# Gated linear attention and a soft mixture of experts on one core: first block by halves, a new schedule table

## The chip, the cores and the metric

The kernel runs on one core of a Trainium2 chip. A core has five engines that work beside each other, each through its own list of instructions in order: TensorE (PE, with its weight loads as PEld), VectorE (DVE), ScalarE (ACT), GpSimd (POOL) and SyncE (SP), which here issues all DMA transfers. The metric is device time in microseconds of one execution; the time before is 164.95 us, the median of 3 runs (164.65 to 165.14).

## What is computed

```python
# _attn_ref: B, H, S, D = 4, 8, 768, 48
f = 1.0 / (1.0 + np.exp(-f_logit))
for t in range(S):
    state = f[:, :, t, :, None] * state + k[:, :, t] outer v[:, :, t]
    y[:, :, t] = q[:, :, t] times state
# y is reordered to x: 3072 x 384
# _moe_ref: 8 experts of 4 slots, F = 1024
logits = x @ phi                       # 3072 x 32
d = softmax of logits over the tokens
slot_input = d.T @ x                   # 32 x 384
slot_out[e] = np.maximum(slot_input[e] @ w1[e], 0.0) @ w2[e]
c = softmax of logits over the slots
return c @ slot_out                    # 3072 x 384
```

(The two lines of the loop and the two softmax lines are shortened.) Everything is 32-bit floating point.

## The kernel before

**Blocks.** The attention is cut into 24 blocks (`NN`): 6 stretches of 128 time steps for each of 4 batches, all 8 heads of a batch in one block. The decay inside a block is turned into running sums of logarithms, so that a block is a few matrix products and a state handed on to the block four later.

**Gates** (`gates`, lines 478 to 506). ACT takes exp (L495, with a sum of its outputs kept for a flag, which costs an ACTIVATION_READ_ACCUMULATOR) and ln (L498) of the gate inputs; DVE scans each block in two runs of 256 columns (L487, L488); ACT takes exp of the sums (`g`, L501) and of their negatives (`p`, L502). Blocks 0 and 1 have gates of 512 columns each, later ones 1024 for a pair of blocks.

**Block** (`block`, L508 on). Two multiplies of 512 columns, `mk` (keys by `g`, L524) and `mq` (queries by `p`, L527), on POOL or DVE; `tk` turns the keys (L532, four transposes), `pk` evicts them (L535), `kv` (L553) builds the block's share of the state, `sa` and `sm` (L557, L562) add and scale it; `ie` (L572) applies the old state to the queries, `sc` (L541) makes the scores, `mask` (L544, DVE) masks them, `ia` (L581) applies them to the values, `py` (L584) evicts. `turn_y` turns the result (`tx` L612, `px` L615). Every fourth block `unit` adds logits, the token softmax in running form, and the slots' inputs (L630 to L665).

**Tail.** From the last unit the slots' inputs are summed (`psi` L752, evicted by DVE as `si` L757); then come `up` (L788), relu, turning, `dn` (L822), a sum over experts (`so` L834) and the combination with the other softmax (`cb` L845), in three parts of the columns; `pf` (L854 to L859) copies the result for the stores. `slots` makes the softmax over the slots (L699 to L714).

**A flag.** The fast way is right only where the gates stay in bounds. `flag1` (five DVE operations, L898 to L902), `flag2` (a transpose, L905) and `flag3` (three small DVE operations, L908 to L910) reduce that to one number; at the end every engine reads it and branches over a slow general version.

**Start.** While the first loads land, eight steps called `warm` (L426) keep TensorE busy, each of two products of 128 x 128 ones (two records a product in the trace).

**The order.** The program has no order written by hand. Each step is given to a planner (`Plan`) with its possible engines and their planned durations, the tiles that it reads and writes, and a due time (`prio`). `schedule` simulates the engines: again and again it takes the step that can begin first; among steps that could begin within `WINDOW` of each other the lower `prio` wins. The list that comes out is the program's order on all engines, the loads on SP's queue included. The table `LATER` shifts due times by kind of step and by an index; `ENGINE` fixes the engine of some kinds (A ACT, D DVE, P POOL, - or an engine that the step can't use: free choice). The index is the first number in the step's name, below 4 as it stands, above that 4 + x % 4:

```python
            x = x if x < 4 else 4 + x % 4
            op["prio"] += LATER[kind][x] if kind in LATER else 0.0
            e = ENGINES[ENGINE[kind][x]] if kind in ENGINE else None
```

The planner's model also has a price for a change of the kind of product on TensorE (`SWITCH`), for every 256 instructions that TensorE fetches (`FETCH`), and a rate for DMA. None of these prices is a wait on the chip: only the order and the choice of engines go into the program.

## Time and profile before

| | us |
|---|---|
| median of 3 runs | 164.95 |
| the profiled execution, its own time | 164.98 |
| its span, first to last instruction | 163.2 |
| TensorE busy (x2461) | 147.3 |
| DVE busy (x234) | 120.3 |
| ACT busy (x186) | 99.0 |
| POOL busy (x43) | 26.2 |

The mean granted clock of TensorE is 0.987. Times of the profile are counted from the start of the span. Its rows give the start, the duration, the engine, the line of the kernel, the operation, output and inputs with their shapes, and a count; in brackets the time that the engine stood idle before it and what ended that. "PE" and "PEld" are products and weight loads of TensorE; a product of 32-bit numbers appears as two records. DMA moved 54.01 MB at a mean of 331 GB/s.

### The profile page before, as it was taken

What the parts mean: (1) busy time and instruction counts of PE and PEld (TensorE: products, weight loads), DVE (VectorE), ACT (ScalarE), POOL (GpSimd) and SP (SyncE); (2) the same over time, 40 slices, a digit from 0 to 9 for tenths busy, and PEclk for the clock granted to TensorE, in tenths of its full rate; (3) what the DMA queues carried; (4) which work ended last, traced back from release to release, by engine and by line L of the source; (5) the groups of instructions that cost most, each with busy time, mean ns of one, the idle gap of its engine ahead of it and who ended that gap; (6) DMA issues with size and microseconds to landing.
All of it is one profiled execution on the core that took longest, in us unless ns stands there. A gap on an engine that the chain in (4) does not pass through costs nothing.

```text
span 163.2 us, 5865 instructions
## 1 busy us (share of the span) xinstructions
PE 147.3 (90%) x2461; PEld 112.6 (69%) x2461; DVE 120.3 (74%) x234; ACT 99.0 (61%) x186; POOL 26.2 (16%) x43
## 2 busy tenths in 40 slices
PE   2998999999999999999999999999999999999600
PEld 2987777688877797878877887778753248777300
DVE  6789998899999999989999999999371113250410
ACT  4998977796959888783886967743440130033520
POOL 4001111050305020060306322160011000000000
PEclk9999999999999999999999999999999999999995
DMA  4999999999999799999999988618999998046891
GB/s 149 346 404 386 407 419 398 383 374 413 390 377 381 267 381 368 382 329 350 387 407 375 319 315 253 241 24 353 428 426 420 420 418 345 16 180 231 332 375 66
DMA packets 17571, 54.01 MB, mean 331 GB/s; under 512 B 1920, under 2 KB 5120, under 8 KB 14464
## 3 DMA queue, kind: packets, MB, share of 16 engines
q1 hardware_dynamic: 17536, 53.55, 87.0%
q8 instruction: 21, 0.34, 0.8%
q14 instruction: 14, 0.11, 0.2%
HBM read 48.82 MB, written 4.72 MB: 328 GB/s over the span
## 4 chain that ended last, share of the span: by engine, by line
PE 61%; DVE 14%; ACT 8%; DMA 7%; issue 3%; SPq 2%; POOL 1%; ACTq 0%; DVEq 0%; POOLq 0%
PE pr L541 12%; PE pr L581 6%; PE sg L612 6%; PE pr L572 5%; PE pr L788 5%; PE sg L822 5%; DVE as L544 4%; DMA ag<-in_f_dram 4%; PE sg L630 3%; PE sg L532 3%; PE pr L845 3%; DMA aq<-in_q_dram 3%; PE sg L659 2%; PE sg L553 2%; PE pr L822 2%
## 5 line engine op out<-in xcount | busy, mean ns | idle before, releaser
L544 DVE TENSOR_TENSOR as<-pr,tri 128x1024 f32<-128x1024 f32 x24 | 29.1, 1214 | 2.2 <-PE pr L541 1.5
L541 PE MATMUL pr<-aq,ak 48*128 48x128 f32 x384 | 27.9, 285 | 0.4 <-DVE as L544 0.2
L541 PEld LDWEIGHTS pr<-aq,ak 48*128 48x128 f32 x384 | 23.3, 187 | 5.0 <-issue 2.5
L581 PE MATMUL pr<-as,av 128*48 128x128 f32 x384 | 24.1, 274 | 1.2 <-DVE as L544 1.0
L581 PEld LDWEIGHTS pr<-as,av 128*48 128x48 f32 x384 | 20.2, 123 | 2.9 <-DVE as L544 2.1
L612 PE MATMUL sg<-ident,xT 128*128 128x128 f32 x96 | 15.2, 282 | 0.4 <-ACT ag L535 0.2
L527 POOL TENSOR_TENSOR aq<-aq,ac 128x512 f32<-128x512 f32 x9 | 11.4, 1281 | 25.0 <-ACT ac L502 8.7
L584 ACT COPY xT<-pr 128x512 f32<-128x512 f32 x20 | 11.5, 582 | 5.5 <-PE pr L581 5.4
L524 POOL TENSOR_TENSOR ak<-ak,af 128x512 f32<-128x512 f32 x6 | 7.7, 1279 | 35.3 <-ACT af L501 23.4
L572 PE MATMUL pr<-aq,st 48*48 48x128 f32 x320 | 13.1, 278 | 0.2 <-DVE aq L527 0.2
L502 ACT ACTIVATE ac<-ac 128x1024 f32<-128x1024 f32 (+1 forms) x13 | 12.9, 993 | 0.5
L612 PEld LDWEIGHTS sg<-ident,xT 128*128 128x128 f32 x96 | 10.4, 141 | 3.6 <-issue 1.5
L854 ACT COPY hm<-pr 128x768 f32<-128x768 f32 x7 | 5.5, 802 | 10.9 <-PE pr L845 10.9
L532 PE MATMUL sg<-ident,ak 128*128 128x128 f32 x80 | 11.9, 282 | 0.0
L487 DVE TENSOR_TENSOR_SCAN ac<-chain,af 128x256 f32<-128x256 f32 x16 | 10.9, 681 | 1.1 <-issue 1.1
L535 ACT COPY ag<-sg 128x512 f32<-128x512 f32 x17 | 9.4, 586 | 3.7 <-PE sg L532 3.7
L615 ACT COPY xr<-sg 128x384 f32<-128x384 f32 x17 | 8.1, 479 | 4.9 <-PE sg L612 4.8
L488 DVE TENSOR_TENSOR_SCAN ac<-chain,af 128x256 f32<-128x256 f32 x16 | 10.6, 665 | 0.0
L553 PEld LDWEIGHTS sg<-av,ag 128*48 128x48 f32 x320 | 8.6, 124 | 2.7 <-issue 1.2
L527 DVE TENSOR_TENSOR aq<-aq,ac 128x512 f32<-128x512 f32 x15 | 10.2, 685 | 0.3 <-POOL ak L524 0.2
L572 PEld LDWEIGHTS pr<-aq,st 48*48 48x48 f32 x320 | 8.0, 119 | 3.4 <-issue 2.0
L532 PEld LDWEIGHTS sg<-ident,ak 128*128 128x128 f32 x80 | 8.6, 141 | 2.2 <-issue 0.9
(142 smaller groups left out, 243.0 us busy)
## 6 DMA issues: line engine op xcount, KB each, us to landing
hm<-in_w_dram SPq DMA_DIRECT2D x17, 1024.0 KB, 8.0
ak<-in_k_dram SPq DMA_DIRECT2D x24, 256.0 KB, 5.9
aq<-in_q_dram SPq DMA_DIRECT2D x24, 256.0 KB, 5.8
av<-in_v_dram SPq DMA_DIRECT2D x24, 192.0 KB, 5.4
af<-in_f_dram SPq DMA_DIRECT2D x7, 512.0 KB, 5.6
out_dram<-hm SPq DMA_DIRECT2D x8, 384.0 KB, 3.8
ag<-in_f_dram SPq DMA_DIRECT2D x4, 512.0 KB, 5.9
out_dram<-hm SPq DMA_DIRECT2D x2, 768.0 KB, 4.3
```

The source lines that it names most:

```text
L487: nc.vector.tensor_tensor_scan(cx[:, : 2 * BT], chain, lx[:, : 2 * BT], 0.0, op0=ALU.mult, op1=ALU.add)
L502: add(f"p{n}", {"ACT": t_act(w)}, lambda e: nc.scalar.activation(flat(c_), flat(c_), AF.Exp, scale=-1.0), w=cs, prio=T(n, 1.2))
L527: tt(e)(flat(q_), flat(q_), flat(c_), op=ALU.mult)
L532: nc.tensor.transpose(pk[:, a], k_[:, a], ident)
L541: nc.tensor.matmul(ps[:, r, a], k_[rows[r], col(a)], queries(r, a), start=True, stop=True)
L544: tt(e)(sc_.rearrange("p r (m x) t -> p (r m) (x t)", x=2), bank(("sc", n)).rearrange("p r (m t) -> p (r m) t", m=2), tri.rearrange("p x t ...
L553: nc.tensor.matmul(pk[rows[r], col(a)], kp_[:, col(a), rows[r]], v_[:, 2 * a + r], start=True, stop=True)
L572: nc.tensor.matmul(py[at : at + D, r, a // 2], s0[rows[r], col(a)], queries(r, a), start=a < 2, stop=False, skip_group_check=True)
L581: nc.tensor.matmul(py[at : at + D, r, a // 2], v_[:, 2 * a + r], sc_[:, r, a], start=first and a < 2, stop=a >= 2, skip_group_check=True)
L584: copy(e)(xT[:, n % NXT].rearrange("p (r m) t -> p r (m t)", r=2), bank(("y", n))[:, :, : 2 * BT])
L612: nc.tensor.transpose(px[:, i], xT[:, n % NXT, i], ident)
L822: nc.tensor.matmul(po[32 * qq : 32 * qq + 32, :w], hT[:, j, 4 * kh + kk, 32 * qq : 32 * qq + 32], t[:, qq, kk], start=(j, kh, kk) == (0, 0 ...
```

## The change

Six things are changed together.

1. Block 0's gates are done by halves: a new function `half_gates` takes exp, ln, one scan of 256 columns, `g` and `p` for each half by itself, and `mk0`, `mq0` become four multiplies of 256 columns. `tk0`, `sc0` and the state wait for both halves.
2. Five warming steps instead of eight.
3. The flag's three steps move behind `slots` in the program, and `flag1` now waits for `si` (the slots' inputs).
4. The tables: `LATER` and `ENGINE` have 16 indices instead of 8 (0 to 7 as they stand, then 8 + x % 4, and 4 more from 20 on), all values are new, from a new search; `WINDOW` is 0.13 instead of 0.21.
5. The planner's prices: `SWITCH` by kind of product, `FETCH` 5.3 while DMA is loaded and 3.6 else, a dearer DMA between 3 and 5 us, transposes counted as half as many instructions, and new durations for `warm`, `tk`, `tx`, `te`, `ie`, `pi` and the flag.
6. TensorE's branch hint stands ahead of `cb00` (the first combination) instead of `dn23` (the last `dn`).

```diff
-WINDOW = 0.21
+WINDOW = 0.13
...
-    "mk": (20.3, 14, 24.2, 9.4, 17.6, -18.3, 17.3, -7.9), "mq": (7.6, -23.3, 11.9, -6.7, 16.8, 17.1, 12.7, 7),
+    "mk": (18.4, 23.4, 11.4, 16.8, 25, 23, 24.7, 18.4, 24.8, 13.7, 25, 22.9, -19.9, 4.1, -4.5, 3.4),
+    "mq": (1, -2.1, -18.8, -7.9, 20.5, 23.6, 22.4, 18.8, 23.1, 18, 20.4, 16.1, -9.4, 4.4, 19.8, 0.8),
...
-    "ends": "AA--DDDD", "mk": "--DP-PDA", "mq": "AA--D---", "pc": "-APAPPPP", "pe": "-PA-----", "pf": "PAADAAAD",
-    "pk": "-AA--P--", "plt": "--D-PPPP", "ps": "DD--DDDD", "px": "D-APA-PP", "py": "A-APPPA-", "relu": "DA----PA",
-    "sml": "A-P-AAAA", "ssb": "D-P-PPPP",
+    "ends": "PA--ADDDAD-DDDDD", "mk": "DAA-D-DA-PA-PDDD", "mq": "D-AD--D-DAP-PAAA", "pc": "PDAADDDDDDDDDDDD",
+    "pe": "AD--ADDDDDDDDDDD", "pf": "APAAPPPPPAD-P-PP", "pk": "ADPAPDP---PPPPPP", "plt": "ADPDAAPPPPPPPPPP",
+    "ps": "ADP-AAAAAAAAAAAA", "px": "AD-PA-D---A-DDAP", "py": "-D-PD-P-APPAPPP-", "relu": "AP--AAAAAA--AAAA",
+    "sml": "PDD-DDDDDDDDDDDD", "ssb": "AD--------------",
...
-    LAT, PE_LAT, SWITCH, DMA_LAT, RATE, DEPTH = 0.13, 0.17, 0.19, 2.0, 375e3, 8
-    INS, PAGE, FETCH = 4, 256, 5.8
+    LAT, PE_LAT, DMA_LAT, RATE, DEPTH = 0.13, 0.17, 2.0, 375e3, 8
+    SWITCH = {"turn": 0.07, "col": 0.1, "half": 0.22, "row": 0.13, "slot": 0.16, "comb": 0.1, "sum": 0.1, None: 0.1}
+    INS, PAGE, FETCH, IDLE = 4, 256, 5.3, 3.6
...
-            x = x if x < 4 else 4 + x % 4
+            x = x if x < 8 else 8 + x % 4 + (4 if x >= 20 else 0)
...
-                    page = max(end - rest, page + self.FETCH)
+                    page = max(end - rest, page + (self.FETCH if pipe > page + 1 else self.IDLE))
...
-                pipe = max(pipe, t + self.DMA_LAT) + op["bytes"] / self.RATE
+                pipe = max(pipe, t + self.DMA_LAT)
+                pipe += op["bytes"] / self.RATE * (3 if 3 < pipe < 5 else 1)
...
-    for x in range(8):
-        add("warm", {"PE": 0.3}, warm(x), r=["ones", "kv0"], w=["warm"], prio=100, form="turn", products=2)
+    for x in range(5):
+        add("warm", {"PE": 0.75}, warm(x), r=["ones", "kv0"], w=["warm"], prio=100, form="turn", products=2)
...
+        def half_gates(h, ex):
+            lh, ch = fb[0][:, 0, 2 * h : 2 * h + 2], cb[0][:, 0, 2 * h : 2 * h + 2]
+            F_, C_, sub = ks[0], cs[0], lambda k: (*k, "half", h)
...
+            act("exp", t_act(w2) + 0.1, lambda e: nc.scalar.activation(lh, lh, AF.Exp, scale=-1.0, accum_out=esum[:, ex : ex + 1]), [F_], [sub(F_), ("es", h)], T(0, -3))
+            act("ln", t_act(w2), lambda e: nc.scalar.activation(lh, lh, AF.Ln, bias=1.0), [F_], [sub(F_)], T(0, -2.5))
+            add(f"scan0.{h}", {"DVE": t_scan(256)}, scan_, two=True, r=[F_, sub(F_), C_, "chain"], w=[sub(C_)], prio=T(0, -1))
+            act("g", t_act(w2), lambda e: nc.scalar.activation(lh, ch, AF.Exp), [F_, C_, sub(C_)], [sub(F_)], T(0, 1))
+            act("p", t_act(w2), lambda e: nc.scalar.activation(ch, ch, AF.Exp, scale=-1.0), [C_], [sub(C_)], T(0, 1.2))
...
+            both = {"POOL": t_pool(256), "DVE": t_dve(256)}
+            for h in range(2):
+                at = slice(2 * h, 2 * h + 2)
+                add(f"mk0.{h}", both, mul(k_, g_, at), two=True, r=[K, G, (*G, "half", h)], w=[HK[h]], prio=T(n, 2))
+                add(f"mq0.{h}", both, mul(q_, c_, at), two=True, r=[Q, CB, HC[h]], w=[HQ[h]], prio=T(n, 2.1))
...
-    add("flag1", {"DVE": 0.8}, flag1, r=["esum"], w=[("pend", n) for n in range(NN)], prio=T(NN, 20))
+    add("flag1", {"DVE": 2.6}, flag1, r=["esum", ("es", 0), ("es", 1), "si"], w=[("pend", n) for n in range(NN)], prio=T(NN, 20))
...
-    hints = {"si": [EN.SP, EN.Pool, EN.Activation, EN.DVE], "dn23": [EN.PE]}
+    hints = {"si": [EN.SP, EN.Pool, EN.Activation, EN.DVE], "cb00": [EN.PE]}
```

More of the change, by code (lines that the diff above doesn't have):

```diff
@@ L587, in block @@
         paced.append(len(plan.ops))
-        add(f"mk{n}", both, mul_k, two=True, r=[G], w=[K], prio=T(n, 2))
-        add(f"mq{n}", both, mul_q, two=True, r=[CB], w=[Q], prio=T(n, 2.1))
+        HK, HQ, HC = ([(*k, "half", h) for h in range(2)] if n == 0 else [] for k in (K, Q, CB))
+        if n:
+            add(f"mk{n}", both, mul(k_, g_), two=True, r=[G], w=[K], prio=T(n, 2))
+            add(f"mq{n}", both, mul(q_, c_), two=True, r=[CB], w=[Q], prio=T(n, 2.1))
+        else:
+            both = {"POOL": t_pool(256), "DVE": t_dve(256)}
+            for h in range(2):
+                at = slice(2 * h, 2 * h + 2)
+                add(f"mk0.{h}", both, mul(k_, g_, at), two=True, r=[K, G, (*G, "half", h)], w=[HK[h]], prio=T(n, 2))
+                add(f"mq0.{h}", both, mul(q_, c_, at), two=True, r=[Q, CB, HC[h]], w=[HQ[h]], prio=T(n, 2.1))
         if not final:
-            add(f"tk{n}", {"PE": 0.4}, turn_k, r=[K, "ident"], psum=("kt", n), kind=("one",), prio=T(n, 3), form="turn", products=4)
+            add(f"tk{n}", {"PE": 0.48}, turn_k, r=[K, *HK, "ident"], psum=("kt", n), kind=("one",), prio=T(n, 3), form="turn", products=2)
             add(f"pk{n}", {"ACT": t_act(512), "DVE": t_dve(512, True)}, put_k, psum=("kt", n), w=[KP], prio=T(n, 3.5))
@@ L615, in put @@
             copy(e)(x_, bank(("xt", n)).rearrange("p (i o e) -> p i o e", i=PR, o=2)[:, :, :, :D])
-        add(f"tx{n}", {"PE": 0.4}, tr, r=[("xT", n % NXT), "ident"], psum=("xt", n), kind=("one",), prio=T(n, 6), form="turn", products=4)
+        add(f"tx{n}", {"PE": 0.48}, tr, r=[("xT", n % NXT), "ident"], psum=("xt", n), kind=("one",), prio=T(n, 6), form="turn", products=2)
         add(f"px{n}", {"ACT": t_act(384), "DVE": t_dve(384, True)}, put, psum=("xt", n), w=[("x", n % NX)], prio=T(n, 6.5))
@@ L715, in slots @@
         for u in (2 * th, 2 * th + 1):
-            add(f"ct{u}", {"PE": 0.11}, turn(u), r=[L, "ident"], psum=("ct", u), kind=("one",), prio=sp + 0.5, form="turn", products=1)
+            add(f"ct{u}", {"PE": 0.11}, turn(u), r=[L, "ident"], psum=("ct", u), kind=("one",), prio=sp + 0.5, form="turn", products=0.5)
             add(f"pc{u}", {"ACT": 0.28, "DVE": 0.25}, put(u), psum=("ct", u), w=[("cts", u)], prio=sp + 0.6)
@@ L874, in tail @@
                 add(f"relu{j}{hf}", {"ACT": t_act(512), "DVE": t_dve(512, True)}, relu(j, hf), psum=("up", j, hf), w=[H_, *extra], prio=t0 + 1.5)
-                add(f"tn{j}{hf}", {"PE": 0.45}, turn(j, hf), r=[H_, "ident"], psum=("tn", j, hf), kind=("one", "late", "spare"), prio=t0 + 1, form="turn", products=4)
+                add(f"tn{j}{hf}", {"PE": 0.45}, turn(j, hf), r=[H_, "ident"], psum=("tn", j, hf), kind=("one", "late", "spare"), prio=t0 + 1, form="turn", products=2)
                 add(f"ph{j}{hf}", {"DVE": t_dve(512, True)}, put_h(j, hf), r=["emask"], psum=("tn", j, hf), w=[("hT", j, hf)], prio=t0 + 1)
@@ L910, in flag3 @@
         nc.vector.tensor_copy(gbad, gok[:1, 2:3])
-    add("flag1", {"DVE": 0.8}, flag1, r=["esum"], w=[("pend", n) for n in range(NN)], prio=T(NN, 20))
-    add("flag2", {"PE": 0.15}, flag2, r=[("pend", 0), "ident"], psum="flag", kind=("one",), prio=T(NN, 20), products=1)
-    add("flag3", {"DVE": 0.3}, flag3, psum="flag", w=["flag"], prio=T(NN, 20))
     ending = len(plan.ops)
@@ L924, in gla_soft_moe_kernel @@
         slots(th)
+    add("flag1", {"DVE": 2.6}, flag1, r=["esum", ("es", 0), ("es", 1), "si"], w=[("pend", n) for n in range(NN)], prio=T(NN, 20))
+    add("flag2", {"PE": 0.15}, flag2, r=[("pend", 0), "ident"], psum="flag", kind=("one",), prio=T(NN, 20), products=1)
+    add("flag3", {"DVE": 0.6}, flag3, psum="flag", w=["flag"], prio=T(NN, 20))
     spots = list(ARENA.values()) + [(homes[x], [("home", x)]) for x in range(len(W1))]
@@ L1034, in general @@
         for o in plan.order:
-            if o["n"] >= ending:
+            if o["n"] >= ending and o["name"] not in ("flag1", "flag2", "flag3"):
                 o["fn"](o["on"])
```

89 lines of the change are left out of this document (73 added, 16 removed), and 57 rows, old and new, of the table LATER.

## The prediction

> **What bounds the kernel now.** I read the page first, for the time and for who is busy:
>
> ```profile
> span 163.2 us, 5865 instructions
> PE 147.3 (90%) x2461; PEld 112.6 (69%) x2461; DVE 120.3 (74%) x234; ACT 99.0 (61%) x186; POOL 26.2 (16%) x43
> PE 61%; DVE 14%; ACT 8%; DMA 7%; issue 3%; SPq 2%; POOL 1%; ACTq 0%; DVEq 0%; POOLq 0%
> ```
>
> TensorE is busy for 90% of the span and holds 61% of the chain of waits. The profiled execution took 164.98 us, 1.78 us of it outside the span; the median of the runs is 164.95 us, so sums made against 164.98 can be read against the median. About 0.3%, or 0.5 us, is what a measurement of this kernel can tell from no change.
>
> An average says little, so the next view is busy time by stretch. I cut it where the timeline shows a new regime: first score product, the point from which TensorE runs full, last logits, slots' inputs, last product.
>
> ```profile
> 0.00:9.66 9.66, 6.55 (x33) 6.43 (x33) 7.04 (x18) 7.23 (x14) 1.67 (x13) 1.00 0.79 274
> 9.66:18.94 9.28, 7.99 (x118) 6.56 (x117) 8.42 (x14) 8.38 (x15) 1.28 (x1) 1.00 1.06 396
> 18.94:118.50 99.56, 98.18 (x1715) 79.08 (x1716) 92.25 (x173) 72.91 (x139) 22.05 (x27) 1.00 0.94 347
> 118.50:122.90 4.40, 3.95 (x47) 2.16 (x46) 3.48 (x14) 1.84 (x8) 0.69 (x2) 1.00 1.00 417
> 122.90:154.50 31.60, 30.66 (x553) 18.36 (x553) 8.06 (x16) 7.00 (x12) 0.54 (x1) 1.00 0.72 293
> 154.50:163.20 8.70, 0.00 (x0) 0.00 (x0) 1.02 (x2) 1.59 (x3) 0.00 (x0) 0.77 0.61 234
> ```
>
> The columns are stretch, length, busy time of PE, PEld, DVE, ACT and POOL, clock, DMA share and GB/s. From 18.94 to 118.50 TensorE idles 99.56 - 98.18 = 1.38 us in all. There a different order can win little by filling holes; but whatever brings the start of this stretch forward brings everything behind it forward too, as long as data and gates keep up. So the front decides, and I read it instruction by instruction in the timeline:
>
> ```profile
> 3.11 6.62 PE L426 MATMUL sg<-ones 128*128 128x128 f32 x32 [3.11 <-DVE ones L384]
> 3.44 0.63 ACT L495 ACTIVATE af<-af 128x512 f32<-128x512 f32 x1 [1.35 <-DMA af<-in_f_dram]
> 5.52 0.67 DVE L488 TENSOR_TENSOR_SCAN ac<-chain,af 128x256 f32<-128x256 f32 x1
> 6.21 0.63 ACT L501 ACTIVATE af<-ac 128x512 f32<-128x512 f32 x1
> 7.54 0.69 DVE L527 TENSOR_TENSOR aq<-aq,ac 128x512 f32<-128x512 f32 x1
> 8.15 0.68 DVE L524 TENSOR_TENSOR ak<-ak,af 128x512 f32<-128x512 f32 x1
> 9.66 1.16 PE L541 MATMUL pr<-aq,ak 48*128 48x128 f32 x16
> 14.53 1.06 ACT L501 ACTIVATE af<-ac 128x1024 f32<-128x1024 f32 x1 [0.50 <-DVE ac L488]
> 15.67 1.28 POOL L524 TENSOR_TENSOR ak<-ak,af 128x512 f32<-128x512 f32 x1 [11.93 <-DMA aq<-in_q_dram]
> 18.20 0.69 DVE L524 TENSOR_TENSOR ak<-ak,af 128x512 f32<-128x512 f32 x1
> 18.94 0.97 PEld L541 LDWEIGHTS pr<-aq,ak 48*128 48x128 f32 x16 [0.37 <-DVE ak L524]
> ```
>
> Block 0 is one chain: exp, ln, scans, g, p, the two multiplies, the scores. The second multiply ends at 8.15 + 0.68 = 8.83, yet the first score product starts at 9.66 with no idle before it: TensorE was still in its 32 warming records, which end at 9.73. So the warming, not the gates, holds the start now. The third score product, at 18.94, waits for a multiply at the end of another chain (g at 14.53, a multiply on POOL, more on DVE).
>
> **The change, part by part.** Gates by halves and fewer warming products go together. Prices of narrower work stand in groups of other stages:
>
> ```profile
> L712 ACT ACTIVATE ltok<-ltok 128x256 f32<-128x256 f32 x3 | 1.2, 417 | 3.7 <-POOL ltok L711 2.5 <-DVE ltok L711 1.3
> L714 DVE TENSOR_TENSOR ltok<-ltok,cm 128x256 f32<-128x256 f32 x1 | 0.4, 424 | 0.0
> L495 ACT ACTIVATION_READ_ACCUMULATOR af<-af 128x1 f32 x9 | 1.7, 189 | 0.0
> ```
>
> By halves: exp 3.44 to 3.86, accumulator to about 4.0, ln to 4.4; scan 4.5 to 5.1. ACT meanwhile does the second half's exp, accumulator and ln, to 5.4, then g and p of the first half to 6.2, while the second scan ends at 6.1; then g and p of the second half to 7.0. Four multiplies of 0.42 us on DVE, three of them behind 6.1 and the last behind its p at 7.0, end near 7.7. Ready: about 7.8 instead of 8.93 (8.83 and 0.1 for the signal). Five warming adds of two products, two records each, are 20 records instead of 32: 6.62 x 20/32 = 4.1 us, done at 7.3. So the first score product starts at about 7.8, **1.86 us earlier**, and the cover that hid the slow gates is gone: from here the gates are late, not the warming.
>
> Not all of this is won. The warming records become quicker while they run; these two groups are those of the stretches from 3 to 5 us and from 9.3 to 9.6 us:
>
> ```profile
> L426 PE MATMUL sg<-ones 128*128 128x128 f32 x9 | 2.3, 439 | 3.1 <-DVE ones L384 3.1
> L426 PE MATMUL sg<-ones 128*128 128x128 f32 x4 | 0.6, 275 | 0.0
> ```
>
> One takes 439 ns at first and 275 ns at the end, though the granted clock reads 1.00 all along. Nine per two microseconds is 0.22 us each; at that pace the 32 would last 7 us, not 6.62, so the quick ones come only in the last microsecond, from about 8.8. A score product that starts at 7.8 runs its first microsecond at roughly half pace: 0.5 us lost, 1.86 - 0.5 = 1.36. [...]
>
> ACT pays for the halves: four activations of 0.63 us become eight of 0.417 and one more accumulator read, 8 x 0.417 + 0.19 - 4 x 0.63 = 1.0 us more, on an engine that is busy 8.38 of 9.28 us in the second stretch. Where it stands before block 2's exp, the third score product comes up to 1.0 us later; where it fills waits, it costs nothing. The loads don't forbid an earlier one: 9.66 us at 274 GB/s and 9.28 us at 396 GB/s are 6.3 MB by 18.94, while four blocks, of three loads of 256 KB and one of 192 KB each, need 4 x 0.98 = 3.9 MB. The front is then worth between +1.0 and -1.86; I take **-1.2**, near the start's own 1.36, because the 1.28 us multiply on POOL is freed for DVE (0.68) by the new engine table.
>
> The new table with its search reorders all of the middle, the loads on SP's queue too, and nothing in the trace shows the new order. On the gain side stand the 1.38 us of idle time and the changes between kinds of product:
>
> ```profile
> 35.52 0.66 PE L612 MATMUL sg<-ident,xT 128*128 128x128 f32 x4
> 36.16 0.65 PE L572 MATMUL pr<-aq,st 48*48 48x128 f32 x16
> 38.42 1.09 PE L532 MATMUL sg<-ident,ak 128*128 128x128 f32 x8
> 39.44 0.83 PE L541 MATMUL pr<-aq,ak 48*128 48x128 f32 x10
> 44.46 0.65 PE L572 MATMUL pr<-aq,st 48*48 48x128 f32 x16 [0.23 <-DVE aq L527]
> ```
>
> A lone group of four transposes holds TensorE from 35.52 to 36.16, 0.64; two together from 38.42 to 39.44, 0.51 each. There are 24 + 20 such groups; were half of them lone and all paired, 22 x 0.13 = 2.9 us would go, an end that no order reaches because banks and multiplies are due one block at a time. On the other side every instruction in order can wait as at 44.46, 0.23 us. So the middle is worth between -4.3 (both gains) and a loss priced below; I take **-0.7**, half of the idle time, the nearer row.
>
> The flag:
>
> ```profile
> 108.86 0.20 DVE L898 TENSOR_SCALAR pend<-pend 128x96 f32<-128x96 f32 x1
> 109.67 0.16 DVE L902 TENSOR_TENSOR gok<-gok 128x1 f32<-128x1 f32 x1
> 114.22 0.27 PE L905 MATMUL sg<-ident,gok 128*1 128x128 f32 x1
> 114.61 0.82 PEld L581 LDWEIGHTS pr<-as,av 128*48 128x48 f32 x16 [0.31 <-DVE as L544]
> ```
>
> Its five DVE operations last 109.83 - 108.86 = 0.97 us; its TensorE product stands in a hole, since the next product waits for the mask anyway. Behind the slots' inputs DVE is busy 8.06 of 31.60 us and covers the five; TensorE, busy 30.66 of 31.60, takes the product with a change of kind, 0.27 to 0.4, unless it falls in one of the holes of that stretch (0.94 in all). Taking 0.97 us from DVE in the middle gives between 0 and 0.97. The new dependency makes nobody wait: the slots' inputs are copied by DVE itself, just ahead, and what queues behind the flag's last steps there has 23.5 us of idle DVE around it. I set **+0.1** for the flag, between -0.97 and +0.4.
>
> The hint:
>
> ```profile
> L1095 PEldq BRANCH_PREFETCH_HINT  x1: 45/45/45, 149.2 to 149.2; - x1
> L1040 PEldq COMPARE_BRANCH  x1: 2482/2482/2482, 153.6 to 153.6; - x1
> L1040 SPq EVENT_SEMAPHORE  x8: 17/17/17, 161.1 to 161.9; - x8
> ```
>
> TensorE's branch takes 2.48 us and is over at 156.1, SP's last waits end at 161.9. Made quick, it saves nothing: **0**, on the far side of 0 the price below. Last, the free choice of engine for the final copies:
>
> ```profile
> 154.52 1.02 DVE L859 COPY hm<-sg 128x384 f32<-128x384 f32 x2 [1.65 <-PE sg L845]
> 155.27 0.82 ACT L854 COPY hm<-pr 128x768 f32<-128x768 f32 x1
> ```
>
> ACT does three in a row to 155.27 + 0.82 = 156.09, while DVE idles 1.65 us before its own. Spread, they end near 155.9: **-0.2**.
>
> Sum: -1.2 - 0.7 + 0.1 + 0 - 0.2 = -2.0, so 164.98 - 2.0 = **163.0 us**.
>
> **The rivals.** *The start is given back.* ACT's 1.0 us delays block 2's gates and the third score product stays at 18.94; the -1.2 is lost: 164.2. For it speaks ACT's 8.38 of 9.28, against it that the search sees this. *Nothing moves*: the order fills no hole either; then flag and final copies remain, 164.9. *The middle gains more*: all 1.38 of idle time and ten pairs, 1.3, go instead of 0.7: 161.0. Against it: DVE is busy 92.25 of 99.56 us as well.
>
> *Slower by order.* The table fits planned durations, and the chip runs the list in order. If a dozen products wait as the one at 44.46 does, 12 x 0.23 = 2.8 us, 165.8. It decides from nine such waits on, where they eat the 2.0. For it: every engine's order is new at once, and the trace's order is one that leaves only 1.38 us. Against: the new planned prices stand nearer to the rows (a warming add 0.75 instead of 0.3, with 6.62/8 = 0.83 measured; four transposes 0.48 instead of 0.4).
>
> [...]
>
> [...]
>
> **How the numbers follow.** Forecast (161.8 to 164.0) 0.56; gains more 0.10; start given back 0.09, still faster by 0.5%; nothing moves 0.10; array slow 0.03, within 0.3%; slower by order 0.09; hint 0.03. Faster by over 0.3%: 0.56 + 0.10 + 0.09 = 0.75; within: 0.10 + 0.03 = 0.13; slower: 0.09 + 0.03 = 0.12. The range from 161.2 to 165.4 leaves out the slower cases, 0.12, and some half of those that gain more, 0.05. The unknown ends (front +1.0 to -1.86, flag, middle) lie inside it except for the pairing of all transposes.
>
> **What would show it.** Warming of 20 records that ends near 7.3; first score product near 7.8, its 16 records slower than 1.16 us; third score product near 17.7; TensorE's idle time behind it under 1 us; the first product behind the slots' inputs near 121 instead of 122.9; from there to the end 40.3 us as now. A first score product behind 9, or a third one at 18.9 or later, makes the first term wrong; idle time over 3 us in the middle means slower by order; a hole of over 2 us in the tail's products the hint.

## The result, and the profile after

The changed kernel takes 169.79 us (median of 5 runs, 168.52 to 170.45) against 164.95 us (5 runs, 164.45 to 165.14): ratio 1.028, 95% interval 1.024 to 1.032. It is slower; the forecast of 163.0 us and its range are missed. The profiled execution is the fastest of the five, 168.52 us; two runs are at 168.5 to 168.9 us with a mean granted clock of 0.984, three at 169.8 to 170.5 with 0.972 to 0.979. So there are two questions: what costs the profiled execution 3.5 us, and what costs most executions 1.3 more. Times here and below are medians of all executions; a ratio and its interval leave out executions that took over 1.5% longer than the fastest of their kernel.

The page of the profile after, engines and chain:

```profile
span 166.8 us, 5844 instructions
PE 147.8 (89%) x2449; PEld 111.5 (67%) x2449; DVE 123.6 (74%) x241; ACT 96.4 (58%) x182; POOL 32.1 (19%) x47
PE 48%; DVE 18%; issue 6%; ACT 5%; DMA 4%; POOL 1%; DVEq 0%; POOLq 0%; ACTq 0%
```

TensorE is as busy as before, 147.8 us against 147.3, but it holds 48% of the chain instead of 61%, and DVE holds 18% instead of 14%: more of the time is decided by who hands work to TensorE. The timeline of TensorE after, at the front:

```profile
1.99 4.63 PE L468 MATMUL sg<-ones 128*128 128x128 f32 x20 [1.99 <-DVE sg L445]
7.73 1.27 PE L605 MATMUL pr<-aq,ak 48*128 48x128 f32 x16
15.65 1.08 PE L645 MATMUL pr<-as,av 128*48 128x128 f32 x16 [1.71 <-DVE as L608]
17.75 1.16 PE L605 MATMUL pr<-aq,ak 48*128 48x128 f32 x16
20.40 1.16 PE L605 MATMUL pr<-aq,ak 48*128 48x128 f32 x16 [0.41 <-POOL ak L591]
27.81 0.66 PE L596 MATMUL sg<-ident,ak 128*128 128x128 f32 x4 [0.84 <-ACT xr L687]
28.98 1.16 PE L605 MATMUL pr<-aq,ak 48*128 48x128 f32 x16
```

The front came as forecast: first score product at 7.73, third at 17.75, fourth at 20.40 instead of 21.43. The fifth is the turning point: 28.98 instead of 28.41. The same stretches by windows, before (first fence) and after, cut at the first, the fourth, the fifth and the last score product and at the first product behind the slots' inputs:

```profile
9.66:21.43 11.77, 10.23 (x154) 8.39 (x153) 10.83 (x17) 10.84 (x19) 1.28 (x1) 1.00 1.05 398
21.43:28.41 6.98, 6.82 (x125) 5.47 (x125) 6.00 (x11) 4.98 (x11) 1.27 (x1) 1.00 1.01 408
28.41:112.12 83.71, 82.85 (x1468) 66.58 (x1464) 80.39 (x149) 63.59 (x121) 20.79 (x26) 1.00 0.93 335
112.12:122.91 10.79, 10.22 (x142) 7.36 (x138) 6.95 (x25) 3.73 (x11) 0.70 (x2) 1.00 1.01 422
```

```profile
7.73:20.40 12.67, 9.52 (x144) 7.70 (x144) 12.43 (x21) 10.93 (x19) 1.28 (x1) 1.00 1.05 391
20.40:28.98 8.58, 7.57 (x128) 6.04 (x128) 8.18 (x16) 6.36 (x13) 0.00 (x0) 1.00 1.04 414
28.98:115.19 86.21, 83.81 (x1457) 66.99 (x1453) 79.51 (x143) 62.05 (x115) 28.96 (x32) 1.00 0.95 350
115.19:126.86 11.67, 10.81 (x148) 7.81 (x149) 8.15 (x26) 3.10 (x9) 0.00 (x0) 1.00 1.01 422
```

From the fourth score product on, the three last stretches are 1.60, 2.50 and 0.88 us longer, 4.98 in all. Length less TensorE's busy time gives its idle time: 0.16, 0.86 and 0.57 before, 1.01, 2.40 and 0.86 after, 2.68 more. The other 2.30 us are more busy time for nearly the same number of products. Behind the last row the tail is 39.94 us instead of 40.29. So -1.03 (front) + 4.98 (middle) - 0.35 (tail) = +3.6, the difference of the spans. Of the tail's 0.35, the products give 0.47 (their last one starts 31.09 us behind the first before, 30.62 after); from the last product to the end it is 9.2 us before and 9.3 after. The DVE column of the first row has changed as well: 10.83 us of 11.77 before, 12.43 of 12.67 after.

The waits of TensorE between the fifth score product and the slots, from the trace of the changed kernel (in order: us in all, times, longest), the four largest:

```profile
PE pr L605 <- DVE as L608: 0.7, 2, 0.5
PE sg L723 <- ACT av L720: 0.5, 2, 0.3
PE sg L824 <- DVE pin L735: 0.5, 1, 0.5
PE sg L723 <- DVE av L706: 0.5, 2, 0.3
```

They are score products behind a mask (L605), the turning of the token softmax (L723) and the last sum of the slots' inputs (L824), each waiting for a step on DVE or ACT. In the kernel before, the same view has four waits of 0.2 us. Busy time per line, for the same number of products, rises for intra products (20.5 us against 19.8), the turning of the token softmax (3.6 against 3.1), state products (8.3 against 7.9) and key transposes (9.3 against 8.9), and falls for inter products (12.3 against 12.7).

### The profile page after: what moved, and what is told of

The parts are those of the page before. It is cut to its first block, busy times and chain, and to the rows that moved or that the text cites. A ratio compares the mean times of both kernels' runs of the same rounds, so it can differ in the third digit from the quotient of the medians.

```text
span 166.8 us, 5844 instructions
## 1 busy us (share of the span) xinstructions
PE 147.8 (89%) x2449; PEld 111.5 (67%) x2449; DVE 123.6 (74%) x241; ACT 96.4 (58%) x182; POOL 32.1 (19%) x47
## 4 chain that ended last, share of the span: by engine, by line
PE 48%; DVE 18%; issue 6%; ACT 5%; DMA 4%; POOL 1%; DVEq 0%; POOLq 0%; ACTq 0%
PE pr L645 9%; PE pr L605 7%; PE pr L860 5%; DMA ak<-in_k_dram 4%; PE sg L894 4%; DVE as L608 4%; PE sg L684 4%; PE pr L636 3%; PE pr L917 3%; PE sg L596 2%; PE pr L894 2%; DVE ac L529 2%; DVE ac L530 2%; DVE sg L621 2%; PE sg L860 2%
## 5 line engine op out<-in xcount | busy, mean ns | idle before, releaser
L605 PE MATMUL pr<-aq,ak 48*128 48x128 f32 x384 | 28.0, 285 | 1.3 <-DVE as L608 0.7
L605 PEld LDWEIGHTS pr<-aq,ak 48*128 48x128 f32 x384 | 23.4, 187 | 5.9 <-DVE as L608 1.7
L645 PE MATMUL pr<-as,av 128*48 128x128 f32 x384 | 24.8, 276 | 2.7 <-DVE as L608 2.7
L591 POOL TENSOR_TENSOR ak<-ak,af 128x512 f32<-128x512 f32 x10 | 12.9, 1296 | 52.4 <-PE pr L605 14.0
L648 ACT COPY xT<-pr 128x512 f32<-128x512 f32 x21 | 12.2, 583 | 15.0 <-PE pr L645 15.0
L596 PE MATMUL sg<-ident,ak 128*128 128x128 f32 x80 | 13.1, 291 | 1.3 <-ACT xr L687 0.8
L591 POOL TENSOR_TENSOR aq<-aq,ac 128x512 f32<-128x512 f32 x10 | 12.6, 1275 | 2.9 <-PE sg L776 2.9
L569 ACT ACTIVATE ac<-ac 128x1024 f32<-128x1024 f32 (+1 forms) x12 | 12.3, 1022 | 0.4
L617 PE MATMUL sg<-av,ag 128*48 128x48 f32 x320 | 10.5, 211 | 0.0
L529 DVE TENSOR_TENSOR_SCAN ac<-chain,af 128x256 f32<-128x256 f32 x15 | 10.2, 681 | 0.2
L599 ACT COPY ag<-sg 128x512 f32<-128x512 f32 x15 | 8.5, 583 | 3.0 <-PE sg L617 2.3
L591 DVE TENSOR_TENSOR aq<-aq,ac 128x512 f32<-128x512 f32 (+1 forms) x15 | 9.4, 650 | 0.9 <-ACT ac L569 0.5
L530 DVE TENSOR_TENSOR_SCAN ac<-chain,af 128x256 f32<-128x256 f32 x15 | 10.0, 667 | 0.0
```

Of the source, the lines that this page charges most:

```text
L529: nc.vector.tensor_tensor_scan(cx[:, : 2 * BT], chain, lx[:, : 2 * BT], 0.0, op0=ALU.mult, op1=ALU.add)
L530: nc.vector.tensor_tensor_scan(cx[:, 2 * BT :][:, ::-1], chain, lx[:, 2 * BT :], 0.0, op0=ALU.mult, op1=ALU.add)
L569: add(f"p{n}", {"ACT": t_act(w)}, lambda e: nc.scalar.activation(flat(c_), flat(c_), AF.Exp, scale=-1.0), w=cs, prio=T(n, 1.2))
L591: return lambda e: tt(e)(flat(x[:, at]), flat(x[:, at]), flat(y[:, at]), op=ALU.mult)
L596: nc.tensor.transpose(pk[:, a], k_[:, a], ident)
L605: nc.tensor.matmul(ps[:, r, a], k_[rows[r], col(a)], queries(r, a), start=True, stop=True)
```

## The experiments

In those that change an order, the planner's simulation is replaced by a list (`ORDER`) with every step's name, occurrence and engine; PSUM banks go to a step in turn, the one idle longest first. The programs keep all work, and differ from the kernel named only as shown. A run's time is its median; "5th to slots" is the time from the fifth score product to the first product behind the slots' inputs; starts and spans are of the profiled execution.

| run | us (lowest to highest) | 1st score | 4th | 5th | 5th to slots | slots to end | span |
|---|---|---|---|---|---|---|---|
| before | 164.95 (164.45 to 165.14) | 9.66 | 21.43 | 28.41 | 94.50 | 40.29 | 163.2 |
| after | 169.79 (168.52 to 170.45) | 7.73 | 20.40 | 28.98 | 97.88 | 39.94 | 166.8 |
| e1_old_middle | 170.42 (169.23 to 171.85) | 7.85 | 21.94 | 32.17 | 94.49 | 41.64 | 168.3 |
| e2_new_middle | 170.27 (169.72 to 170.50) | 9.49 | 21.60 | 30.77 | 97.94 | 39.79 | 168.5 |
| e3_six_to_dve | 170.78 (170.34 to 171.81) | 7.79 | 21.82 | 30.47 | 98.19 | 41.44 | 170.1 |
| e4_warm8 | 170.06 (168.41 to 170.99) | 8.76 | 22.66 | 31.31 | 98.03 | 39.96 | 169.3 |
| e5_front_alone | 168.00 (167.82 to 168.43) | 7.82 | 24.23 | 31.21 | 94.50 | 40.49 | 166.2 |
| e6_front_and_tail | 170.42 (168.16 to 170.71) | 7.87 | 24.72 | 31.70 | 95.79 | 41.41 | 168.9 |
| e7_mask1_first | 174.82 (172.83 to 175.91) | 7.72 | 23.96 | 35.35 | 97.89 | 39.76 | 173.0 |
| e8_flag_back | 170.75 (168.79 to 175.98) | 7.71 | 20.25 | 28.90 | 98.34 | 39.76 | 167.0 |
| e9_fill_hole | 170.60 (169.32 to 172.07) | 7.81 | 21.20 | 29.84 | 97.88 | 40.98 | 168.7 |
| e10_warm5_only | 165.76 (164.76 to 167.51) | 8.81 | 21.83 | 28.81 | 94.50 | 40.89 | 164.2 |
| e11_front_fill_tail | 168.52 (167.35 to 169.56) | 7.74 | 22.45 | 31.38 | 95.80 | 40.02 | 167.2 |
| e12_gates_first | 170.79 (170.40 to 172.07) | 7.74 | 21.79 | 31.21 | 97.83 | 39.86 | 168.9 |
| e13_kv_beside_ia | 169.54 (169.27 to 172.03) | 7.77 | 20.37 | 29.01 | 98.69 | 39.70 | 167.4 |

Beside e1 to e4 the kernel before took 165.17 us, beside e5 to e8 165.49, beside e9 to e11 165.13, beside e12 and e13 165.21.

### The order of the middle: e1 and e2

e1 is the changed kernel with its own order up to the fourth score product and the old one behind it; e2 is the kernel before with the new order behind that product.

```diff
 e1, behind sc3 of the changed kernel:
-w12 scan4 tk3 q7 ia2 mask3 pk3 kv3
+w12 tk3 pk3 scan4 px1 kv3 ln6 sm3
...
 e2, behind sc3 of the kernel before:
-scan5 k6 kv2 mask3 q7 ia2
+ln6 px1 w12 scan4 q7 mask3
...
```

> The changed program (halves, five warming steps, flag behind the slots' inputs, hint at the first combination), but every step behind the fourth score product stands in the order and on the engine that it had before the change. If the new order of the middle is the whole loss: the stretch from the fourth score product to the first product behind the slots' inputs falls from 106.5 us (20.40 to 126.86) back to 101.5 (21.43 to 122.90 before), the front keeps its 1.0 us, and the time is 163.5 to 164.5, below the kernel before. If the flag, the hint or the shorter warming cost the time: 168 or more, since all three are still in it.

> The mirror: the kernel before (whole gates, eight warming steps, hint at the last down product) up to its fourth score product, and from there the order and the engines of the changed kernel. If the order of the middle is the loss: about 5 us over the kernel before, 169 to 171, with warming and front as before. If the front, the flag's dependency or the hint are the loss: 165 to 166.

e1: 170.42 us, ratio 1.028 (1.020 to 1.036). e2: 170.27 us, ratio 1.029 (1.023 to 1.035). Windows from the fifth score product to the slots, e1 (first fence), e2:

```profile
21.94:32.17 10.23, 7.47 (x129) 5.89 (x129) 7.22 (x13) 6.39 (x12) 1.28 (x1) 1.00 0.99 388
32.17:126.66 94.49, 92.87 (x1604) 73.85 (x1600) 86.17 (x165) 67.28 (x132) 21.53 (x28) 1.00 0.89 330
```

```profile
30.77:128.71 97.94, 94.71 (x1605) 74.92 (x1601) 87.60 (x169) 65.18 (x124) 28.93 (x32) 1.00 0.96 352
```

The long stretch goes with the list, which fixes the order and the engine of every step: 94.49 us behind the new front and 94.50 behind the old one with the old list, 97.88 and 97.94 with the new one. Order and choice of engines are changed together here, so their shares stay open. TensorE's own busy time moves with it, 92.87 against 94.71 us. In e2 the stretch from the fourth to the fifth score product is longer too, 9.17 us instead of 6.98. e2 came as expected. e1 as a whole did not: the join of the two orders takes 10.23 us from the fourth to the fifth score product, 6.98 in the kernel before. What the old order gives behind it is shown; that the new front and the old middle add up is not.

### Multiplies on GpSimd: e3

The changed kernel has 23 multiplies on POOL instead of 17, and short DVE operations beside them last up to 1.2 us instead of 0.2. e3 puts six of them on DVE.

```diff
+        if o["name"] in ("mk10", "mq10", "mk14", "mq15", "mq18", "mk19"):
+            o["on"] = "DVE"
         o["fn"](o["on"])
```

> The changed kernel in its own order, with six of its POOL multiplies (keys of blocks 10 and 14, queries of 10, 15 and 18, keys of 19) on DVE instead. Each of the six runs beside a short DVE operation that takes 0.65 to 1.21 us instead of 0.16 to 0.21 in the changed kernel's trace, 4.3 us in all over the short form. If DVE's stall behind POOL is what TensorE waits for: 1.5 to 3.5 us under the changed kernel, 166.5 to 168.3, and no stretched short operation is left. If TensorE's own order is the loss: within 0.7 us of the changed kernel, or slower, since DVE has six multiplies of 0.6 us more to do.

170.78 us, ratio 1.032 (1.026 to 1.037); from the fifth score product to the slots 98.19 us instead of 97.88. Five of the six short operations are back near 0.2 us, but DVE is as busy in that stretch as in the changed kernel (87.83 against 87.66 us), since it now does the six multiplies itself. So moving them wins nothing, against the theory; what the stretched operations cost by themselves is not shown. Two windows of this run show something else:

```profile
16.29:19.70 3.41, 3.41 (x36) 2.63 (x34) 2.88 (x6) 3.22 (x7) 0.53 (x1) 0.50 1.06 401
128.93:132.34 3.41, 3.41 (x20) 0.87 (x16) 0.69 (x5) 0.00 (x0) 0.00 (x0) 0.50 1.03 413
```

The granted clock is 0.50 in both, 1.00 right before and behind. In the first the third score product slips from 17.75 to 18.93. e1 shows the same from 15.92 to 19.33 (third score product at 19.40). The profiled executions of the kernels before and after and of e2 show no such stretch while TensorE has work.

### The half clock: e4, e7, e9, e10

First theory: the warming is too short. e4 gives the changed kernel 16 warming products instead of 10.

```diff
-... for _ in range(2)]
+... for _ in range(2 if x < 4 else 8)]
```

> The changed kernel with as many warming products as before (sixteen), the rest of its order as it is. If the array stays slow in some executions because the warming is short: the times, which spread from 168.5 to 170.5 with mean clocks of 0.984 to 0.972, draw together at 168.5 or below. If the warming's length doesn't matter: the first score product starts about 0.9 us later, behind 8.6, and the time is the changed kernel's, 169 to 170.5, with the same spread.

170.06 us, ratio 1.025 (1.018 to 1.033); the clock is 0.50 from 17.64 to 21.05 all the same, behind a hole of 1.92 us in TensorE's work. Warming longer did not prevent it in this execution. Second theory: the hole ahead of block 1's intra product, 1.71 us in the changed kernel, where the mask stands behind four scans on DVE. e7 moves the mask ahead of them:

```diff
- ... sc1 ... scan3 ... scan2 ... mask1 ...
+ ... sc1 mask1 scan3 scan2 ...
```

> The changed kernel with one move: on VectorE the mask of the second block stands ahead of the four scans of blocks 2 and 3 instead of behind them. Theory: the 1.7 us for which TensorE stands still from 13.9 to 15.65 brings the clock down to 0.50 shortly after in most executions, some 1.3 us each. With the hole gone no execution is disturbed: median 168.3 (167.8 to 168.8) instead of 169.8, mean clock .984 or more in all runs. If the dip comes from the short warming and not from the hole, the median stays at 169.3 to 170.3 and the mean clocks stay between .970 and .985.

174.82 us, ratio 1.051 (1.042 to 1.059), the slowest of all. The hole moved and grew, in TensorE's timeline, and the windows behind it show the half clock for three times as long:

```profile
14.67 1.08 PE L621 MATMUL pr<-as,av 128*48 128x128 f32 x16 [0.74 <-DVE as L584]
18.89 0.66 PE L572 MATMUL sg<-ident,ak 128*128 128x128 f32 x4 [3.14 <-DVE ak L567]
```

```profile
16.41:19.82 3.41, 0.93 (x18) 0.75 (x20) 2.23 (x4) 2.70 (x4) 0.00 (x0) 1.00 1.05 399
19.82:30.06 10.24, 10.24 (x108) 8.90 (x104) 7.72 (x14) 5.36 (x9) 1.27 (x1) 0.50 1.03 413
```

With the mask first, DVE waits 1.40 us for block 1's scores, and block 2's scans, and so its gates and multiplies, come later (14.53 instead of 12.05). The hole was moved, not removed. e9 leaves the order and fills the hole with eight products of ones:

```diff
+    def fill(e):
+        for _ in range(8):
+            nc.tensor.matmul(bank("hold")[:, :128], ones, ones, start=True, stop=True)
...
-  ... tx0 ... ia1 ...
+  ... tx0 ... hold ia1 ...
```

> The changed kernel with eight more products of ones on TensorE ahead of the second block's intra product, where it stands still from 13.95 to 15.65; nothing waits for their result. Theory: it is this hole that brings the clock to 0.50 in part of the executions, so with TensorE busy no execution is disturbed there: all runs at 168.3 to 168.9 us with a mean clock of .982 or more, where the changed kernel has 168.5 to 170.5. Rival (the short warming, or the chip, sets the dip): median 169.3 to 170.3 and mean clocks down to .972 as before; a filler that delays the intra product shows as a third score product later than 17.75.

170.60 us, ratio 1.028 (1.022 to 1.033). The six runs in order of time: 169.32 us at a mean clock of 0.982, 169.58 (0.988), 170.45 (0.979), 170.75 (0.976), 171.88 (0.974), 172.07 (0.966). The filler, which needs a bank, waits 0.57 us for a copy on ACT and delays the intra product by 0.92, and the executions still lie far apart. The profiled one, 170.45 us at 0.979, has no half clock as long as TensorE has work:

```profile
8.09:161.69 153.60, 143.94 (x2441) 108.20 (x2441) 118.18 (x225) 90.89 (x169) 30.24 (x33) 1.00 0.88 333
161.69:168.70 7.01, 0.00 (x0) 0.00 (x0) 0.00 (x0) 0.00 (x0) 0.00 (x0) 0.50 0.37 138
```

The clock falls behind the last product; the clock row of every page here ends in a 5 (tenths), and the windows behind the last product have 0.77 over 8.70 us in the kernel before (from 154.50) and 0.68 over 8.40 in the changed one (from 158.40). So the mean clock counts the idle end too: 1 - 0.5 x 7.01 / 168.7 = 0.979. Against the trace of the changed kernel (168.52 us), this execution has lost 0.86 us at its last product (158.34 instead of 157.48) and 1.0 behind it (10.4 us to the end instead of 9.3), where the last four stores take longer to issue, after (first fence) and e9:

```profile
158.18 2.40 SPq L935 DMA_DIRECT2D out_dram<-hm  x4
```

```profile
159.05 3.88 SPq L916 DMA_DIRECT2D out_dram<-hm  x4
```

So an execution can be 1 us longer at its end, and have a lower mean clock, without a half clock in TensorE's work. The column "slots to end" of the table holds this end too. Whether the hole was what brings the half clock, this run doesn't settle. e10 goes the other way, and takes three warming steps from the kernel before. Of the 17 runs of that kernel beside it one took 764.03 us and is set aside; the other 16 have mean clocks of 0.978 to 0.989:

```diff
-... for _ in range(2)]
+... for _ in range(2 if x < 5 else 0)]
```

> The kernel before with five warming adds instead of eight and nothing else: 20 records, over near 6.6, the gates of the first block still end at 8.9, so the first score product starts near 9.0 instead of 9.66. By the forecast's reading (warming holds the start, half pace for the first microsecond) the time is 164.5 to 165.0 us. By the clock theory a hole of 2 us behind the warming keeps the array slow or brings a dip: 165.5 to 167.5 with mean clocks under .980 and a first score product of over 1.6 us.

165.76 us (12 runs), ratio 1.002 (0.999 to 1.005). Timeline and windows of the profiled one, 165.99 us:

```profile
3.11 4.16 PE L426 MATMUL sg<-ones 128*128 128x128 f32 x20 [3.11 <-DVE ones L384]
8.81 1.16 PE L541 MATMUL pr<-aq,ak 48*128 48x128 f32 x16 [1.54 <-DVE ak L524]
```

```profile
6.63:10.04 3.41, 1.87 (x23) 1.56 (x22) 2.59 (x5) 2.70 (x7) 0.00 (x0) 1.00 0.98 375
10.04:13.45 3.41, 3.31 (x21) 2.49 (x22) 3.19 (x5) 3.38 (x6) 0.00 (x0) 0.50 1.04 397
```

The first score product starts 0.85 earlier, but the half clock follows and the second one comes at 14.49 instead of 13.88. Nine of the twelve runs have mean clocks of 0.963 to 0.979 and take 165.29 to 167.51 us; the other three, at 0.981 to 0.986, take 164.76, 164.91 and 165.12, which is where the kernel before is. So the earlier start won nothing here. In the profiled execution (mean clock 0.967) a hole of 1.54 us behind the warming was followed by the half clock; five more of the twelve have means of 0.963 to 0.969, which speaks for the same in them, but they have no trace.

### The new front without the new middle: e5, e6, e11

e5 takes the changed kernel's order up to the first score product and the old one from there, with flag and hint as before; e6 adds the changed order behind the slots' inputs, with flag and hint as after.

```diff
 e5, behind sc0 of the changed kernel:
-q3 exp2 v2 kv0 mask0 g1
+g1 p1 ends1 mq1 exp2 v3 mk1 mask0
...
```

> The changed program's front (gates of the first block by halves, five warming adds) up to and including the first score product, and from there on every operation in the order and on the engines of the kernel before; flag and TensorE's hint where the kernel before has them. The forecast's own front term, -1.2, says 163.8 us (163.2 to 164.3), first score product near 7.8 and every later one 1 to 1.5 us ahead of the kernel before. If what the front wins is given back before the fourth block, it is 164.7 to 165.2. If five warming adds are too few for the array's clock whatever the order behind them, the clock row shows 0.50 for some 3 us between 15 and 22 us and the time is 165.0 to 166.5.

> The run above with the order of the changed kernel also behind the slots' inputs (final copies, flag and hint as the change has them); the middle alone is in the order of the kernel before. Theory: only the middle of the change loses, the stretch behind the slots' inputs is 0.3 to 0.4 us shorter, so 163.4 us (162.8 to 164.0). If the late flag or the moved hint cost what the change's shorter tail wins, it equals the run above within 0.3.

e5: 168.00 us, ratio 1.016 (1.012 to 1.020). e6: 170.42 us, ratio 1.025 (1.018 to 1.033). Both missed. TensorE's timeline and the windows of e5:

```profile
12.29 1.11 PE L572 MATMUL sg<-ident,ak 128*128 128x128 f32 x4 [3.19 <-DVE ak L567]
```

```profile
10.44:13.85 3.41, 1.55 (x8) 1.15 (x10) 2.92 (x4) 3.18 (x6) 0.00 (x0) 0.50 1.04 385
13.85:17.27 3.42, 3.42 (x54) 3.30 (x52) 2.40 (x6) 3.14 (x6) 0.22 (x1) 0.50 1.05 391
31.21:125.71 94.50, 93.07 (x1604) 73.93 (x1600) 87.34 (x173) 67.25 (x132) 21.48 (x28) 1.00 0.92 338
```

Block 0 is served first, so block 1's scans start at 8.24 instead of 6.13; TensorE runs dry for 3.19 us up to 12.29, and from 10.44 on the clock is at half for two windows. From there on the old order runs as in the kernel before (94.50 us). The start of 1.84 us earlier has become a second score product 2.7 us later. The trace of e6 is another 2.7 us longer than that of e5: 0.49 up to the fifth score product, 1.29 in the long stretch, where the old middle meets the new tail, and 0.92 behind it, with a second half clock from 127.47. e11 joins at the fourth score product as e1 does, and goes over to the changed order again behind `si`, with the hole filled and block 3's mask, scans and state add put so that TensorE doesn't stand behind them (the first line is e1's order):

```diff
 sc3
-w12 tk3 pk3 scan4 px1 kv3 ln6 sm3 scan5 mask3 q7 ia2 g4 ...
+w12 tk3 pk3 scan4 px1 ln6 scan5 mask3 q7 ia2 kv3 sm3 g4 ...
```

> The parts that stood up, together: the changed kernel's front up to the fourth score product with the hole filled as in the first run, the order of the kernel before from there to the slots' inputs (the fourth block's mask, scans and state add arranged so that TensorE doesn't stand behind them), and the changed kernel's order behind them. Theory, by sums of the traces: fourth score product at 20.4, fifth at 28.0 to 28.8, 94.5 from there to the first product behind the slots' inputs, 40.0 to the end: 164.3 to 165.1 us, the same as the kernel before or 0.3% below it. If the join costs as much as in the first of these runs (10.2 us from the fourth to the fifth), it is 166.7 or more.

168.52 us, ratio 1.019 (1.014 to 1.024). The join takes 8.93 us (22.45 to 31.38), and the last unit, joined to another tail, 1.3 more. Even the fastest run, 167.35 us at a mean clock of 0.990, is slower than the kernel before. No version of the front that was tried beat it.

### Flag and hint: e8

```diff
-  ... si ct5 flag1 up000 ... dn23 pf00 pf01 flag2 po2 st00 so2 flag3 ...
+  ... te4 flag1 ie23 ... ia22 pp4 flag2 ia23 ... py23 flag3 ...
-"cb00": [EN.PE]
+"dn23": [EN.PE]
```

> The changed kernel with the flag's five operations back on VectorE in the last unit ahead of the last interstate product, its product on TensorE behind the copy of unit 4's slots, and TensorE's hint back at the last down product. Theory: both parts are worth nothing, so 169.8 us, 0.4 either way, and TensorE's last branch again near 2.0 to 2.5 us. The forecast's bounds would allow 169.4 to 170.8: the flag's 0.97 us of VectorE in the middle is a loss if it lies in front of the mask of the last block.

170.75 us as a median of runs that lie from 168.79 to 175.98, too far apart for a ratio; 168.79 us for the profiled one, against 168.52. Its long stretch is 98.34 instead of 97.88 us, its tail 39.76 instead of 39.94. TensorE's branch, after and e8:

```profile
L1112 PEldq COMPARE_BRANCH  x1: 2062/2062/2062, 157.7 to 157.7; - x1
```

```profile
L1088 PEldq COMPARE_BRANCH  x1: 1802/1802/1802, 158.0 to 158.0; - x1
```

The hint moved nothing: the branch takes about 2 us with it in either place, and SP's last waits end later (165.4 against 159.8 for the branch, after). The flag is worth at most some tenths, less than these runs tell apart.

### Two repairs inside the middle: e12, e13

From the fourth to the fifth score product DVE is busy 8.18 of 8.58 us. e12 lets block 4's gates go first there.

```diff
-sc3 ln6 px1(DVE) w12 scan4 tk3 q7 ia2 mask3 pk3 kv3 py2 scan5 ia3 k7 tx2 sm3 py3 scan6 g4 lg0 px2 p4 mk4 ... mq4
+sc3 px1(ACT) ln6 w12 scan4 tk3 q7 ia2 pk3 kv3 py2 scan5 mask3 k7 g4 p4 tx2 ia3 sm3 px2 mk4 mq4 scan6 py3 lg0 ...
```

> The changed kernel with the stretch from the fourth to the fifth score product put in another order: the gates of block 4 go first (on VectorE the scans ahead of the fourth block's mask, block 1's token copy on ScalarE instead of VectorE, the next scan behind the multiplies; on ScalarE g and p ahead of a copy). Theory: with VectorE busy 8.18 of 8.58 us there, the chain mask, scans, g, p, multiply sets the fifth score product, not TensorE; it comes 7.4 to 7.9 us behind the fourth instead of 8.58, and the time is some 0.8 us less, 168.6 to 169.3 as a median. If TensorE's own products or the loads set it, it stays at 8.4 to 8.8.

170.79 us, ratio 1.036 (1.031 to 1.041). Timelines of DVE and TensorE in e12:

```profile
27.33 0.69 DVE L567 TENSOR_TENSOR aq<-aq,ac 128x512 f32<-128x512 f32 x1 [0.17 <-ACT ac L545]
```

```profile
27.82 1.06 PE L678 MATMUL sg<-xT,av 128*32 128x128 f32 x26 [0.56 <-ACT xT L624]
30.04 0.66 PE L572 MATMUL sg<-ident,ak 128*128 128x128 f32 x4 [0.57 <-ACT xr L663]
31.21 1.05 PE L581 MATMUL pr<-aq,ak 48*128 48x128 f32 x14
```

The multiply of block 4's queries starts 5.5 us behind the fourth score product (27.33 - 21.79) instead of 6.8 (27.18 - 20.40): the gates did come forward. But the fifth score product comes 9.42 us behind it instead of 8.58, because block 3's mask, copy, logits and transposes now come later and TensorE waits for their copies. The gates are not the only bound: two chains share DVE and ACT, and here moving one forward moved the other back.

e13 is about TensorE's busy time. In the old middle 15 of 16 state products stand ahead of another state product or an intra product, in the new one 5. Timelines of before (first fence) and after, one of each:

```profile
22.52 0.56 PE L553 MATMUL sg<-av,ag 128*48 128x48 f32 x16
22.91 2.15 PE L581 MATMUL pr<-as,av 128*48 128x128 f32 x32
```

```profile
57.68 0.56 PE L617 MATMUL sg<-av,ag 128*48 128x48 f32 x16
58.17 1.05 PE L605 MATMUL pr<-aq,ak 48*128 48x128 f32 x14
```

From start to start it holds TensorE 0.39 us ahead of an intra product and 0.49 ahead of a score product. Counted in the two lists from the fifth score product to `psi` by the planner's forms (`form`; a step without one counts as its own), neighbours of different form rose from 95 to 104. e13 moves three of the lone ones back.

```diff
-kv13 ie13 sa13 sc13 sm13 ... te2 mask13 ex2 ia12 ...
+ie13 sc13 ... te2 mask13 ex2 kv13 ia12 ... sa13 sm13 ...
```

> The changed kernel with three of its eleven lone state products (blocks 13, 17 and 18) moved back to stand directly ahead of an intra product, and their state add and multiply on VectorE behind them. Theory: a state product takes 0.39 us ahead of an intra product and 0.46 to 0.50 ahead of another kind, and the kind that follows saves its own change: 97.4 to 97.7 us from the fifth score product to the first product behind the slots' inputs instead of 97.88, time 169.5 (169.2 to 169.9). If the changes of kind cost nothing by themselves, it stays at 97.8 to 98.2; if the later state holds up the inter products, it is more.

169.54 us, ratio 1.026 (1.023 to 1.029). The window from the fifth score product to the slots:

```profile
29.01:127.70 98.69, 94.58 (x1604) 74.53 (x1601) 86.32 (x169) 65.52 (x124) 28.94 (x32) 1.00 0.95 355
```

The three state products did take 0.39 us each instead of 0.46 to 0.50; but busy time as a whole stayed (94.58 against 94.62 us in the same stretch after), and idle time rose from 3.26 to 4.11 us. Of the waits, those of score products behind a mask grew most, from 0.7 to 1.2 us. So moving three single products did not bring the old order's grouping, and how much of the 2.30 us of busy time the lost grouping costs is not shown.

## Why the prediction was wrong, point by point

- **The front, -1.2: right in size, its terms less so.** First score product 7.73 (forecast 7.8), third 17.75 (17.7), gain at the fourth 1.03. The warming began at 1.99 instead of 3.11 and ended at 6.62, not 7.3. The first score product's 16 records took 1.27 us instead of 1.16, so the slow start cost 0.11 and not 0.5 (the half pace was an estimate from two rows of the warming; what the traces show is 1.27 us here and 1.16 in e10, behind 20 warming records as well); and 0.90 of the lead of 1.93 went between the first and the fourth score product (12.67 us instead of 11.77), for which the working had 0.16 left. Two errors of opposite sign cancel here, which is in part luck.
- **The middle, -0.7: the step that failed.** It came out at +4.98. The working took TensorE's 1.38 us of idle time as what an order can win, and the price of one wait, 0.23, times a dozen as what it can lose. Both are read from an order in which waits are rare and neighbours are well grouped; neither bounds another order. The traces show 2.68 us more idle time and 2.30 us more busy time, and e1 and e2 that the long stretch goes with the list of order and engines. Against the pairing of transposes, forecast as a possible gain, stands a loss of grouping: in the old order 15 of 16 state products stood beside one of their kind or an intra product, in the new one 5. That this makes the busy time is likely but not shown (e13).
- **The engine that becomes the bound was not worked out.** The text noted DVE at 92.25 of 99.56 us and used it only against a larger gain. Between the first and the fourth score product DVE is now busy 12.43 of 12.67 us (10.83 of 11.77 before). Block 1's scans start at 8.15 instead of 6.13 and block 4's at 20.83 instead of 18.80, while those of blocks 2 and 3 stay (12.05 against 12.01); e5 and e7 show what happens when DVE's order is pushed further. *The start is given back* was priced at third score product; it was given back one step later, between the fourth and the fifth, 1.60 us.
- **Slower by order, 165.8, 0.09**: the right rival. Its dozen waits are there: from the fourth score product to the slots TensorE has twelve of 0.15 us or more, 4.01 us in all, against four of 0.73 in all before. What it lacked is the 2.30 us of busy time, and waits up to 0.84 instead of 0.23 each.
- **The array stays slow, 165.2, 0.03**: this price takes it that products stay slow behind a hole between the warming and the scores. No run shows that: in e10 the first score product, 1.54 us behind the warming, took 1.16 us as in the kernel before. What the runs show is a granted clock of 0.50 later on: in e10 from 10.04 to 13.45, where eight transposes, from 9.90 on, took 2.22 us instead of 1.09. In the profiled execution of the changed kernel the clock reads 1.00 throughout the front, and block 0's transposes (6.41 to 7.60) fill most of the time between the warming's end at 6.62 and the scores at 7.73. In e11, which has the same front, the clock does fall early, from 10.03, behind a stretch (6.62 to 10.03) with the first score product and a wait of 0.8 us for a load; in e1, e3, e4, e7 and e12 it falls later, behind stretches of the same length with TensorE busy 1.70, 1.70, 1.49, 0.93 and 1.69 us. Whether it takes the median from 168.52 to 169.79 has no trace. The median execution's mean clock of 0.972 would need 9.4 us at half clock (0.028 x 168.1 / 0.5), more than the end of any trace here has (7.4 at most, e10: 0.033 x 164.2 / 0.5 - 3.41), which speaks for one drop; the two at 0.978 and 0.979 could come from a long end alone, as in e9.
- **Flag +0.1, hint 0, copies -0.2**: the sum, -0.1, is near the tail's -0.35, but not by its terms. The gain lies in the products (-0.47); the last copy does end sooner behind the last product (1.76 us instead of 2.09), yet the way from there to the end is no shorter (9.3 us against 9.2). The hint did nothing; the price set against it, 5.0 us at a chance of 0.03, is shown by no run: TensorE's branch took 2.06 us in the changed kernel against 2.48, and the longest wait among the tail's products is 0.35 us.

From the forecast to the profiled execution: 163.0 + 5.7 (middle) + 0.2 (front) - 0.3 (tail, against -0.1) = 168.6, measured 168.52; the other 1.3 us of the median are not settled.

What stays open: what the new order and what the new engines cost by themselves, where the 2.30 us of busy time come from, how the largest wait (0.84 at 27.81) can be removed, since e12 only moved the time elsewhere, and what lengthens the changed kernel's longer executions, the half clock or the end behind the last product, since only the fastest of them has a trace.

## What to carry to other kernels

A schedule that leaves TensorE 1.4 us idle in 100 is not to be judged by that remainder when all of it is replaced: count what the old order has achieved (neighbours of one kind, states ready in time) and price the loss of it. Before a stage is brought forward, add up the engine that feeds it: where DVE is full from there to the next stages, the lead is only lent. And don't count on a start that is won by cutting the warming: in e10 it came 0.85 us earlier, behind a hole of 1.54, the clock stood at 0.50 from 10.04 to 13.45, and nothing was won.
